# Transducer joint kernel: the second feature projection and two more groups of joint tiles computed by seven block products

## The chip, the cores and the metric

The kernel runs on one core of a Trainium2 chip. The metric is the time of one execution on the device in microseconds; the kernel before was run three times: 251.55, 252.01 and 252.47 us, median 252.01.

The core's engines, as the profile names them: PE (matmul; PEld is its weight load), DVE (VectorE), ACT (ScalarE), POOL (GpSimd) and SP, which here only issues DMAs. Matmul results stand in PSUM, which has eight banks of 512 fp32 columns; ACT and DVE read them out ("evict" them) to SBUF.

## What is computed

```python
h  = conv5(x, w1)                       # x: (2, 4000, 512), five taps, 512 -> 512
h  = gelu(h)[:, ::2, :]                 # (2, 2000, 512)
f  = gelu(conv5(h, w2))[:, ::2, :]      # (2, 1000, 512)
fe = f @ w_f                            # (2, 1000, 512)
ge = g @ w_g                            # (2, 8, 512)
j  = tanh(fe[:, :, None, :] + ge[:, None, :, :])   # (2, 1000, 8, 512)
out = j @ w_o                           # (2, 1000, 8, 512), bf16
```

All data are bf16. The joint part is the last two lines: 16,000 rows (16 pairs of batch and label position, 1000 rows each) through a 512 x 512 matrix.

## The kernel before

**Convolutions.** The first 216 rows of the first layer are done tap by tap; the rest of both convolutions runs in 24 *units* u0 to u23 (class Unit): six stretches of rows, four blocks of 128 output channels each. A unit has five steps, s1 to s5, of one or two products each; ACT applies GELU to their results. Units u16 to u19 make the features of the first batch (fT[0]) and u20 to u23 those of the second (fT[1]) from hT[1].

**Feature projection.** feT[b] = w_f applied to fT[b]. For the first batch the class Feature (L1001) does it by *seven block products*: both matrices are halved in both directions and seven products of half-size blocks take the place of eight, at the price of sums and differences of blocks. `wfsums` (L996) makes four sums of blocks of w_f (tile fs); `Feature.sums` (L1011) makes four of fT (tile ft); the methods p1 to p7 then do a product each for two blocks m of 128 output channels. Results that are needed twice are copied to sn, and added on DVE to later ones. For the second batch `fe` (L717) does it plainly: eight calls, four matmuls of 501 columns each, one eviction each, on ACT for odd m and on DVE for even m.

**Joint.** `tanh` on ACT makes j from feT and geT, up to 1000 columns at a time, into the rings jT and jX. The 16,000 rows are 125 tiles of 128. A tile is done in one of two ways:
- class Plain (L844): four matmuls of 512 columns into one bank, one eviction to ost, one store of 128 KB. `half` does half of the columns, two halves make a tile.
- class Seven (L873): four tiles at a time, a *group*. Four sums of blocks of j (`Seven.sums` L889, tile ss, on DVE or POOL), then seven products of four matmuls with 256 columns each, against blocks of w_o or their sums (tile tw, `wosums` L988). The bank A takes products 1, 6, 7 and 4 one after the other, the bank D products 5 and 3. Of the seven evictions three are copies to sn (s1, d5, u2; on ACT or DVE), three are additions on DVE to og (c11, c12, c22) and one is a copy to og (c21). A group is stored in two halves of 256 KB.

Before, 29 groups cover 116 tiles (L1135 to L1140) and nine tiles are plain: two at the start of the joint part, two after the 22nd group, two after the 28th, three at the end, the last of them in halves.

**What sets the order of the work.** The code issues operations in a logical order and derives every dependence from the cells that each one reads and writes. The order on each engine is not that of the code: it is read from a table, ORDER (L69), with one string for each engine. Each pair of letters is an operation's number; the table also says on which engine an operation runs that may run on two (evictions on ACT or DVE, sums on DVE or POOL). `schedule` (L198) reads it, `emit` (L210) adds the semaphores. The engines go through their lists strictly in that order. In the code's own order, `piece` (L1108) takes the next step of the list conv (what is left of the units, then the projection of the second batch) and puts it between the steps of the groups; `fill` (L1146) says how many go with each group.

**Ends.** The last three tiles (L1180 to L1195): one plain tile, the first half of the last, product 4 of the last group, the middle tile in halves, the second half of the last, whose eviction ACT does. SP issues all stores, in the table's order.

Of the kernel before, what the change touches and what calls it, by code (L numbers as in the profile page):

```python
# [63 lines left out]
class Op:  # L64
# [6 lines left out]
        "0X0Y0Z0a0b0c0d0e0f0h0j0l0t0u0v0w0x0y0z0_0-101112131415161g1718192C2c1A1i2J1j2K2m2E2e2n2f2F2x2v2M2N2j2p2k302q2y313334"  # L71
        "36373O3J3K3t3H3X3P3R3S3U3h3e3V3Z3a3i414A423k3v3l3_3w4K4C4D4L3f3-4Y444a454b4i4H4I4v4N4O4f4l5L4o4j5p4g4q5V4r4w4y4z4-4m"
        "505z5S5N5_5W5O6N5r5Y5Z5s5T6O6L6l606Y615w6Z6V5x6v6S6w786W6s6T6n6o7R7I6t7A7B7b6y7J7p7c7F6z7L7G7T7Y7U7r7Z7s7e7f7M807z81"
        "7_8T838m8A7w857x8B868D8E8n8d8e8V8W8r8a8t8G8u8g8H8h8-8o908p8y8z9D9F8b9G929N9K939Q9R9L9T9U9O9f9o9h9j9k9y9v9q9xA3A7A2A0"
        "A9ABAHAKAEAIAfANAgALASAiAjAlAmAPAvAwBGAoApB7B8AyBABBB0AzBgB1BQBTBDBHBRBhBEBmBJBUBKBnBdBpBqBjBsBkBXByCEBYC7BzCFBeB-C8"
        "CKCLCHCQCIC3CRC0CNC4CgCZCcCaCtCuCmCdChCzDACODBCnCwC_D3CxDLD0DPDQD1DSD4DHDVDIDbDDDTDcDEDYDlDiDmDWDZDjDvE6DwE3E4DpEZEC"
        "E7E0E1EDEaEQE9DqEJEKEUEAEMEVEREcEdENEfEiErEjEgEsF2EyEuFGFHFAEzElEvFJFBFDFKFdFEFSFMFTFZFaFVFjFWFkFpFsFmFnFvFqF-GNG2G0"
        "G3FtGEG6G7GFGjGKGHGLGOGkGIGWGQGXG-GdGeH0GsGmGnGpGZGqGaHCHLHDGvGtHIHFHGHJH2H6H7HUHMHjHkH3HVHXHOHbHcHmHsHYHtHpHnHzH_Hq"
        "IMIGIjIHINIPI0IkIJIKIQI4IdIpI1I5IWIZIXIqIeIzIaJCI_ImInJDJ4JfJIJJJFIsJGJSJ0JgJ5ItJ1JLJZJVJTJWJoJMJpJvJiKAJjJwKJKBJlJa"
        "JyKGJzJmKHKDKQKEKnKRKKKhK0K1KqKiKTKrKULALBKxKkKoKyKXKlLJLKKYLDLQLRLGK_K-LEL2LHLjLgL3LdLeLhLTLXLmLkLULwLYLnM9LxLpMILz"  # L80
        "L_M3M4MAMFMCMGMDMJMjMkMLMVMSMpMTMZNCMqMaMsNDMWMzMmMnNIM_NhNLNiMtN0NSN4NTNJNFNGN1NnN5NkNoNxNyNMNlO2NVNWO8NZNqNrOBOCN_"
        "N-O3OENaO9OHOIOFOkOlOOOPOROVOWOSOeP3P4OhObOfOcOnOuOvP9OiPAOxOyP6PCP7O-PJP0PFPKPMPNPDPTPUPQPRPXPaPdPePhPjPm"),
    "act": (
        "080k1L1F0m1N1s1o1y1R1Q1P1B1_1C1h1D2D2d1q1a1k2L1E1c2o2S2w2O2i2l2I2U2r2X352W2-323B383I2Y3Y3T3Q3p3u3D3n3j3W3o4B434S3N3d"
        "4M404Z3m3z3g464P4U5M4p4k544J4e4G5q52534_4h5-5X4n4x65514u5a5U6m6M71675y5R5K6-5v6X6a6R6U626x79707S7K7j7H7d5o6u7l6_5J7q"
        "7g6K7N6r827a7-7E848U6D8O5n5h7v6J7X8C8F6k898f7y8s6j8N978I8P918q778_8Z9E8c6d8i8x999M9S949V9J9P9g9p9i9z9r9nA49-AZA6ADAG"
        "AbAOAMAaAeAcAqAQB6AdAJB5BiBSCpCABLCsCCBVBtCBCrCDB_C9BfDOCqC1CbCvDND-CeB4CoCUDCD_DMDREYEXF8DdDnD5F4F5FgDzF7FfEEGCELFh"
        "EWF9GiFiGDF6EtHgEwFCHfFeIEFNHiIFFlGhHhG4G1JAK7GlJBGYIhIBGbK6IAGwK8K9HKHlJdHPIDICKdH-HrIOIlIiKbI2IrIbI-JeKgJKJhJ2KfJX"
        "L9JxKcL8JnM8KeKIKjM7LCMhLcKpLSMgLIL0LfLbLlNfLqLyNBN8MfMHNgMUNAMrNEMXN9M-NjNUNpNKNzMiNXO7O0OAOQO6OTOdP5OoPBOzPGPOPYPf"
        "PkPn"),  # L90
    "dve": (
        "000g0i1I1J1m1M1K1O1n1l1w1r1p1x1v1G1S1z1X1H1-1U1T2Q1V1W1Y1u1Z1b1f2R1d2G1e2H2g2P2h1t2T2z2t2V2_2b2Z2a2s3L3M3C392u3A3q3G"
        "3b3E3F3c493r3s3x4R473y4E4c4d4F4Q4T484V4s4t555d4W64574X565P5c66725t7P6P635u5Q5b5G5H5g5k6Q5E6A7Q69735F685I6p7i6G756q5i"
        "7C7D745l6B5f7O7k5j7V7W5m7t6c6H7h6C7o6E7u6F7m6g6I6e7n6h6b76876f888X8Q6i8S8Y8R8v8w988k8j9C8l969a9W9H9I959e9Y9B9Z9A9t9s"
        "9b9u9l9m9w9_A8A5A1AAACAFAXAVAWATAhAkAtBOAxAnArBMAsB9BCA_B2BIBFB3BoBrCVCWBlBuBZBvCGCMCJCSCTDeC5CPDfCiDhC-CyD9EFD2DUDJ"
        "DFDXDkDaDxDyE5E8E2FODrEBEbEOEeEhESF3EkE_EmFIF_FFFLFUFbGyFoFXFrFwFuGGG8GMGJGPGRGfH1JQHTHvGrGoHEGuHHH8H4HWHNHdJtHZHuHo"
        "ISIvITIIILI6IYIRIfIoJEJPJHJ6JsJUIuJNJkJqKCJ_JbKFKSK2KLKtKVKzKmKZKsLFLPLtL4LiLLMOLZLVLoM5MBMEL-MKMlMMMbMoMxNOMuNPNtNH"
        "N2N6NNNmNuNsNvNwOKODOGOJNbO4OXOgOsOwOjOmP8P1PLPEPVPSPbPi"),
    "pool": (
        "01020304050n0o0p0q20210r0s5e8M9X9d9cAYAuBNCXBPBwD8BxCYDgD6D7EHEGEnEIEoEpEqFxFQFyFPFzFRGSGTGVGUGxG_GzHQHRIxHSHwHxKOHy"  # L100
        "IUKvIwIVJOJrIyKMJuLMJRKNKPLsKuLNKwLvMvLOLuMwMPMRMyMQNRNQOLOMONOqOrOt"),
    "sp": (
        "0607090A0B0C0D0E0F0G0H0I0J0K0L0M0N0O0P0Q0R0S0T0U0V0W22232425262728292A2B58595A5B5C5D8J8K8LARAUA-BWBaBbBcC2C6CfCjCkCl"
        "DGDKDoDsDtDuEPETExE-F0F1FYFcG5G9GAGBGcGgH5H9HAHBHaHeI3I7I8I9IcIgJ3J7J8J9JYJcJ-K3K4K5KWKaL1L5L6L7LWLaLrM0M1M2M6MNMYMc"
        "MdMeN3N7NYNcNdNeO1O5OUOYOZOaOpO_P2PHPIPPPWPZPcPgPlPo"),
# [178 lines left out]
def bass_standalone__seq2seq_rnn_t_joint__speech_kernel(  # L284
# [22 lines left out]
    NK = D // P  # L307
# [3 lines left out]
    NT3 = (T2 + 2) // 3  # L311
# [5 lines left out]
    NT = 512  # L317
    NWARM = 8

    with ExitStack() as es:  # L320
# [396 lines left out]
        def fe(b, half, m):  # L717
            q = NT3 // 2
            v = ps.cols(bank(), 3 * q)
            mm(v, [(wf_sb[k, m * P:(m + 1) * P], fT[b][k, :, half * q:(half + 1) * q]) for k in range(NK)], True, True)  # L720
            v = v.map(lambda a: a.rearrange("p (r q) -> p q r", r=3))
            o = feT[b][m, 3 * half * q:3 * (half + 1) * q].map(lambda a: a.rearrange("p (q r) -> p q r", r=3))
            if m % 2:
                act(o, v, ACT.Copy)
            else:
                pl.op("dve", lambda e, o=o, v=v: e.tensor_copy(out=o.ap, in_=v.ap), (v,), (o,), vec_cost(o, (v,)))  # L726

# [268 lines left out]
        def wfsums():  # L996
            a11, a12, a21, a22 = (wf_sb[2 * k:2 * k + 2, m * H:(m + 1) * H] for m in range(2) for k in range(2))
            for i, x, y, op in ((0, a21, a22, add), (1, fs[0], a11, sub), (2, a11, a21, sub), (3, a12, fs[1], sub)):
                shared(fs[i], x, y, op, True)

        class Feature:  # L1001


            def __init__(self, b):
                self.b = b
                lo = (slice(0, FQ), slice(NT3 - FQ, NT3))
                self.B = {(k, n): fT[b][2 * k:2 * k + 2, :, lo[n]] for k in range(2) for n in range(2)}
                self.r = {1: (0, 0), 2: (1, 0), 3: (1, 1)}
                self.bk, self.kept = {}, {}

            def sums(self, late):  # L1011
                f = self.B
                for i, x, y in (((1, f[1, 1], ft[0]), (2, f[1, 1], f[0, 1]), (3, f[1, 0], ft[1])) if late else ((0, f[0, 1], f[0, 0]),)):
                    shared(ft[i], x, y, sub, False)

            def product(self, i, m, start):
# [7 lines left out]
                if lhs is None:  # L1024
                    s = {5: 0, 6: 1, 7: 2, 3: 3}[i]
                    lhs = lambda k: fs[s, k, c]
                if i in self.r:
                    kh, n = self.r[i]
                    lo = n * (NT3 - FQ)
                    rhs = lambda k: fT[self.b][2 * kh + k, :, lo:lo + FQ]  # L1030
                else:
                    t = {5: 0, 6: 1, 7: 2, 4: 3}[i]
                    rhs = lambda k: ft[t, k]
# [66 lines left out]
        wfsums()  # L1100
# [5 lines left out]
        conv += [lambda h=h, m=m: fe(1, h, m) for m in range(NK) for h in range(2)]  # L1106
# [40 lines left out]
        Plain(plains.pop(0)).go()
        Plain(plains.pop(0)).go()
# [31 lines left out]
        if len(plains) == 3:  # L1180
            Plain(plains[0]).go()
            end = Plain(plains[2])
            end.half(0, "dve", "sp")
            seven[-1].p4()
            Plain(plains[1]).halves()
        else:
            for j in plains[:2]:
                Plain(j).go()
            seven[-1].p4()
            for j in plains[2:-1]:  # L1190
                Plain(j).halves()
            end = Plain(plains[-1])
            end.half(0, "dve", "sp")
# [31 lines left out]
```

## Time and profile before

| | |
|---|---|
| runs, median (lowest to highest) | 252.01 us (251.55 to 252.47) |
| profiled execution, whole time | 251.88 us |
| its span, first to last instruction | 250.1 us |
| mean granted TensorE clock | 0.997 |
| matmuls with 256 columns | 828 |
| additions og <- acc, sn on DVE | 87 |
| sums ss on DVE, on POOL | 42, 74 |
| tanh on ACT from one pair and 128 channels | 64, in 84 pieces |
| last matmul ends, in the span | 246.44 us |
| median time from the issue of a 256 KB store to its landing | 2.2 us |

How to read it: the page gives the busy time of each engine as a share of the span, the chain of work that ended last, followed back from the last instruction, and the costliest groups of instructions. A group's line names the source line, the engine, the operation, the tiles (written <- read), the shape and the number; helpers record most operations, so that the matmuls all have line L411, DVE's additions L397, ACT's activations L403, copies of results L826 (ACT) and L827 or L831 (DVE), sums for groups L895 and the other shared sums L983. A record's duration includes latency that overlaps the next record; the time from one start to the next is what an engine that never waits spends on an operation.

### The profile page before, as it was taken

To read this page: it belongs to the slowest core of one execution; us is meant where nothing else is said; L and a number is where in the kernel's file an instruction comes from. 1 tells how busy PE (TensorE), PEld (TensorE's weight loads), DVE (VectorE), ACT (ScalarE), POOL (GpSimd) and SP (SyncE) were. 2 spreads that over 40 slices of the span, in tenths; PEclk is the share of its full clock that TensorE was granted. 3 is DMA by queue.
4 is the path that set the end of the run, shared out by engine and by line. 5 is a ranking of instruction groups with operands and counts; after the bars stand their busy time and mean duration, and the time that the engine had idled before them with its cause. 6 is when DMAs were issued, how large, how long until landed. Compare 5 with 4: busy or idle time off the path is not lost.

```text
span 250.1 us, 5178 instructions
## 1 busy us (share of the span) xinstructions
PE 244.3 (98%) x1912; PEld 184.1 (74%) x1916; DVE 216.3 (86%) x376; ACT 207.6 (83%) x351; POOL 90.1 (36%) x96
## 2 busy tenths in 40 slices
PE   8999999999999999999999999999999999999994
PEld 4556888887666666666558787877878888888873
DVE  1699989775999999799979867988999999979982
ACT  2199699848669398987899989999999999997853
POOL 1000000000000000001414494999857988695730
PEclk9999999999999999999999999999999999999998
DMA  7999999982900520000001123323333445564377
GB/s 218 323 205 181 184 164 185 165 144 84 321 19 3 182 70 3 1 1 3 0 0 66 63 87 127 126 87 128 126 116 116 141 161 187 168 197 164 100 251 240
DMA packets 57392, 31.92 MB, mean 128 GB/s; under 512 B 33837, under 2 KB 57149, under 8 KB 57367
## 3 DMA queue, kind: packets, MB, share of 16 engines
q1 hardware_dynamic: 57367, 31.59, 48.3%
q8 instruction: 15, 0.25, 0.4%
q14 instruction: 10, 0.08, 0.1%
HBM read 7.71 MB, written 16.38 MB: 96 GB/s over the span
## 4 chain that ended last, share of the span: by engine, by line
PE 98%; ACT 0%; issue 0%; DVE 0%
PE acc L411 97%; PE acc L489 1%; ACT xs L403 0%; ACT ost L403 0%; DVE zero L418 0%
## 5 line engine op out<-in xcount | busy, mean ns | idle before, releaser
L397 DVE TENSOR_TENSOR og<-acc,sn 128x512 bf16<-128x512 f32 x87 | 57.2, 684 | 6.5 <-PE acc L411 6.2
L411 PE MATMUL acc<-tw,ss 128*128 128x256 f16 x348 | 54.1, 273 | 0.0
L403 ACT ACTIVATE jT<-feT,geT 128x1000 bf16<-128x1000 f32 (+6 forms) x56 | 51.2, 950 | 0.4 <-DVE feT L726 0.3
L411 PEld LDWEIGHTS acc<-tw,ss 128*128 128x128 f16 x348 | 33.7, 98 | 6.7 <-ACT sn L826 0.3
L826 ACT ACTIVATE sn<-acc 128x512 f32<-128x512 f32 (+1 forms) x56 | 32.5, 617 | 4.8 <-PE acc L411 4.7
L411 PE MATMUL acc<-wo_sb,jT 128*128 128x256 bf16 (+1 forms) x192 | 33.8, 286 | 0.4 <-ACT jT L403 0.3
L411 PE MATMUL acc<-row,w_sb 128*128 128x334 bf16 (+1 forms) x192 | 32.1, 295 | 0.0
L411 PE MATMUL acc<-row,w_x 128*128 128x262 bf16 (+1 forms) x192 | 28.8, 290 | 0.0
L393 POOL MEMSET hT<- 128x8 bf16 (+2 forms) x6 | 0.7, 149 | 76.2 <-ACT hT L403 71.0
L403 ACT ACTIVATE sd<-acc 128x334 f32<-128x334 f32 (+1 forms) x48 | 19.9, 430 | 8.2 <-PE acc L411 7.8
L895 POOL TENSOR_TENSOR ss<-jT 128x512 f16<-128x512 bf16 x20 | 23.6, 1183 | 6.4 <-ACT jT L403 3.5
L403 ACT ACTIVATE jX<-feT,geT 128x1000 bf16<-128x1000 f32 (+4 forms) x28 | 25.1, 937 | 0.0
L411 PEld LDWEIGHTS acc<-row,w_sb 128*128 128x128 bf16 x192 | 18.5, 97 | 6.4
L411 PEld LDWEIGHTS acc<-row,w_x 128*128 128x128 bf16 x192 | 18.5, 98 | 6.1 <-ACT sd L403 0.4
L411 PEld LDWEIGHTS acc<-wo_sb,jT 128*128 128x128 bf16 x196 | 18.9, 98 | 5.2 <-ACT jT L403 0.4
L895 POOL TENSOR_TENSOR ss<-jT,ss 128x512 f16<-128x512 bf16 x15 | 17.3, 1158 | 11.7 <-DVE ss L895 11.5
L403 ACT ACTIVATE hT<-acc 128x262 bf16<-128x262 f32 (+2 forms) x36 | 15.2, 433 | 6.1 <-PE acc L411 6.1
L411 PE MATMUL acc<-wo_sb,ss 128*128 128x256 bf16 x116 | 20.3, 273 | 0.0
L827 DVE COPY sn<-acc 128x512 f32<-128x512 f32 x27 | 18.3, 684 | 1.4 <-PE acc L411 1.3
L500 DVE SCALAR_TENSOR_TENSOR acc<-acc,sd 128x334 f32<-128x334 f32 (+1 forms) x24 | 11.6, 485 | 6.6 <-ACT hT L403 3.2
L411 PE MATMUL acc<-hT,w_sb 128*128 128x334 bf16 x96 | 17.1, 305 | 0.0
L411 PE MATMUL acc<-row,w_t 128*128 128x334 bf16 x96 | 16.6, 305 | 0.0
(120 smaller groups left out, 503.8 us busy)
## 6 DMA issues: line engine op xcount, KB each, us to landing
out_dram<-og SPq DMA_DIRECT2D x44, 256.0 KB, 2.2
w_sb<-in_w_dram SPq DMA_DIRECT2D x9, 512.0 KB, 5.2
out_dram<-og SPq DMA_DIRECT2D x14, 128.0 KB, 2.2
out_dram<-ost SPq DMA_DIRECT2D x7, 128.0 KB, 2.2
xr<-in_x_dram SPq DMA_DIRECT2D x1, 512.0 KB, 3.6
w_sb<-in_w_dram SPq DMA_DIRECT2D x2, 256.0 KB, 4.8
wf_sb<-in_w_f_dram SPq DMA_DIRECT2D x1, 512.0 KB, 3.6
wg_sb<-in_w_g_dram SPq DMA_DIRECT2D x1, 512.0 KB, 4.6
```

The costliest lines, as they stand in the source:

```text
L393: pl.op("pool", lambda e: e.memset(v.ap, 0.0), (), (v,))
L397: pl.op(eng, lambda e: e.tensor_tensor(out=o.ap, in0=a.ap, in1=b.ap, op=op), (a, b), (o,), 0.02 + 2.14e-3 * o.ap.free_size() if eng == "po ...
L403: pl.op("act", lambda e: e.activation(o.ap, i.ap, func, scale=scale, bias=0.0 if bias is None else bias.ap), rd, (o,), o.ap.free_size() * ...
L411: ins = e.matmul(o.ap, lhsT=l.ap, rhs=r.ap, start=start and n == 0, stop=stop and n == len(pairs) - 1, skip_group_check=not check)
L489: ins = e.transpose(pv.ap[:, r, k, :], xr[rt].h[0:n, 2 * r + pp, k, :], ident.h[0:n, 0:n])
L500: pl.op(eng, lambda e: e.scalar_tensor_tensor(out=o.ap, in0=a.ap, scalar=f, in1=b.ap, op0=ALU.mult, op1=add), (a, b), (o,), vec_cost(o, (a ...
L826: pl.flex({"act": (lambda e: e.activation(o.ap, v.ap, ACT.Copy), 0.05 + n * 0.833e-3), "dve": (lambda e: e.tensor_copy(out=o.ap, in_=v.ap) ...
L827: "dve": (lambda e: e.tensor_copy(out=o.ap, in_=v.ap), 0.065 + n * 1.04e-3)}, (v,), (o,))
L895: fn = lambda e, o=S[i], x=x, y=y, op=op: e.tensor_tensor(out=o.ap, in0=x.ap, in1=y.ap, op=op)
```

## The change

Three things change; the convolutions and everything before the joint part are the same.

1. The projection of the second batch is done by the class Feature too. The function `fe` goes. ft and fs become lists of two; the second pair lies in hT[1], whose rows are read last by units u20 to u23. `wfsums` is called a second time for the second pair.
2. The groups begin at tile 0 and cover 124 tiles in 31 groups. One plain tile is left, the last one, in two halves. The steps "p" that put plain tiles between groups go.
3. The order table is another one. It has 1700 operations for 1651.

```diff
-        ft = at("ft", [4, 2, 3, FQ], BF16, ss[1].end - ss[1].bytes)
-        fs = at("fs", [4, 2, NT // 2], FP16, ss[3].end - ss[3].bytes)
-        assert ft.end <= ss[2].end
+        ft = [at("ft0", [4, 2, 3, FQ], BF16, ss[1].end - ss[1].bytes), at("ft1", [4, 2, 3, FQ], BF16, hT[1].end - hT[1].bytes)]
+        fs = [at("fs0", [4, 2, NT // 2], FP16, ss[3].end - ss[3].bytes), at("fs1", [4, 2, NT // 2], FP16, ft[1].end)]
+        assert ft[0].end <= ss[2].end and fs[1].end <= hT[1].end
...
-        conv += [lambda h=h, m=m: fe(1, h, m) for m in range(NK) for h in range(2)]
+        f1 = Feature(1)
+
+        for m in range(2):
+            conv += [lambda m=m: (f1.p1(m), m or (f1.sums(False), wfsums(fs[1]), f1.sums(True))),
+                     lambda m=m: (f1.p5(m), f1.p2(m)), lambda m=m: (f1.p6(m), f1.p3(m), f1.c12(m)),
+                     lambda m=m: (f1.p7(m), f1.p4(m))]
...
-        S1 = 15
-        gaps = (6, 12)
-        NEND = ntile - (2 + 4 * S1 + 4 * 14 + 2 * len(gaps))
-        jts = [2 + 4 * i for i in range(S1)]
-        j = 2 + 4 * S1
-        for n in range(14):
-            jts.append(j)
-            j += 4 + 2 * gaps.count(n)
-        assert jts[-1] + 4 < ntile
+        jts = [4 * i for i in range(ntile // 4)]
+        NEND = 1
         seven = [Seven(j) for j in jts]
-        plains = [j for j in range(ntile) if not any(q <= j < q + 4 for q in jts)]
-        fill = ["cc"]*9+["c"]*6+["p"]*15
-        Plain(plains.pop(0)).go()
-        Plain(plains.pop(0)).go()
+        plains = [ntile - 1]
+        fill = ["cc"]*9+["c"]*6+[""]*16
...
-        if len(plains) == 3:
-            Plain(plains[0]).go()
-            end = Plain(plains[2])
-            end.half(0, "dve", "sp")
-            seven[-1].p4()
-            Plain(plains[1]).halves()
...
+        end = Plain(plains[0])
+        end.half(0, "dve", "sp")
+        seven[-1].p4()
         end.half(1, "act", "sp")
```

Operations of the joint part by engine, counted in the two tables:

| | before | after |
|---|---|---|
| PE, products of 256-column blocks (two matmuls each) | 406 | 434 |
| PE, 504-column products (two matmuls each) | 14 | 28 |
| PE, 501-column products (four matmuls each) | 8 | 0 |
| PE, plain tiles: 512 columns / 256 columns (four matmuls each) | 7 / 4 | 0 / 2 |
| DVE, 512-wide additions / copies | 87 / 49 | 93 / 42 |
| DVE, feature additions / copies (501 and 504 wide) | 6 / 6 | 12 / 4 |
| DVE, sums for groups / for features / of weights | 42 / 4 / 5 | 57 / 8 / 8 |
| ACT, 512-wide copies / feature copies | 74 / 10 | 82 / 12 |
| POOL, sums for groups / of weights | 74 / 3 | 67 / 4 |
| SP, stores | 97 | 94 |

More of the change, by code (lines that the diff above doesn't have):

```diff
@@ L70 @@
     "pe": (
[L71 to L82, printed above, removed]
@@ L83 @@
-    "act": (
[L84 to L90, printed above, removed]
@@ L91 @@
-    "dve": (
[L92 to L98, printed above, removed]
+        "0X0Y0Z0a0b0c0d0e0f0h0j0l0t0u0v0w0x0y0z0_0-101112131415161718191g1A2C2c1i1j2m2v2J2n2K2E2F2x2e2f2y2M2p2N362q333O2j3730"
@@ new lines @@
+        "34312k3H4A3X3J3K3t3R3P3S3h3i413Z423a3e3f4C4D4K3v3U4N3w3V3k4L3_3l4Y444a4b453-4H4o4O4i4l4m5L4j4I5p4q4r4y5V4f4z4v4-5W4g"
+        "6L4w5S5N5O505z5r5s5_5T6l6N5Y5w5Z5x6O786v6V606W6S617I6Y6T7J6w6Z6s6n6o7T7A6t7p7B7R6y7U7L7F7M6z7G7e7f837b7Y7c7Z7z7r7_8D"
+        "7w8E85867s8T8V80818A7x8m8d8W8B8e8n8o8a8r8t8G8b8H8g8-8h908p8u8y9D9F8z929K9G9N939O9f9Q9R9L9T9U9h9o9v9xA09y9qA3A7ANA9A2"
+        "9jAiAEAj9kABB1AZAwAxAHAaB2AKALAIApAcAdAfBDAqBVBABEBWAsB4AgB5BKBkAtBYBBB7BLBZBNBOB8BeBfBhBqBrBbBcBRC8BSCBBzC9C1C2BiCE"
@@ new lines @@
+        "CTCUCFBtBuCCCHCoCICpB_CaCWCbCXCKCLD5DJClCmDKD6DFCxCuCyCvD2CrD3DVCsDWCeCfDBDMDNDCDnDPDcDQDdDfDuDoDvDjDgDxE4DyDkEODSEB"
+        "DTE5EEEFE1ETEZE2EUEaD_D-ECEPEfE_EKE-EcEWELEtEuEXEdF2FCF4FFEwExFGFQFOFxFDFrFsFZFIFyFWFXFJFjG7FaFuFLFvFfFMG8FgGEFlGFGA"
+        "GBGKG1GTGLGNF_F-GUGOGYGeGtGQGRGWH3GfGzGuG_GhGnGwGxGiH5HBHYHEH0HCH1GoHFHxHMHPHNHVHaHSHTHIHQHJI1HgI2HhHyHjHWHpIYHqHkH_"
+        "IBICH-ISI4I5IxIbITIZIIIVIcIJIWIEIiIyIjJ1JOJPIFIrIsJ2JBJCJUJVI_JeI-JIIlJfJJJRImJEJSJ4JnJFJtJuJ5JoJXK0KMK7K8JhJYJwKNJi"
@@ new lines @@
+        "JxJzJ_K1KSKTKtKuKPKEKFKcKVKQKWKdKAKzLKK_KlLLKBKfKgL7LELaL8LFL0KmKwKxLQL1LbLRLNLpLALBLOLTLqLsLtMILjMJLUM3LkM4LvLyLzLd"
+        "MYLeLwMZM6M7MlMRMrMmMOMLMPMAMMMBMSMuM-N0MsMfMgMoMpNGNHMbMcNMN6MvN7NNNJNKNWN2N3OENPNlNmOFNXNZNrNdNaNeNQN-O0NsNoNuNpNv"
+        "OUOKOLOHOhOVOiO2OnO3OoOIO6OxO7OyObOcOkOqOlP8ONOrP9OOOXP2PBPCOYPEP3O_POO-PPPHPFPZPRQ0PSPcQ1PdPaPIPVPfPiPWPgPjPpPqQCQD"
+        "PsPwPxPtQ3Q4Q6Q7Q9QJQAQFQGQKQMQNQQQTQUQX"),
+    "act": (
+        "080k0m1o1N1L1q1R1Q2S1P1s1B1y1h1_2d1C1k2D1a1D2o2L1c2w1F1E2U2r2O2W2X35382Y2l3Y2i3I323B3u3T2I433D3N4B3j3g3n3d3o3W3Q4M2-"
+        "3z3m3p464Z404S5M4P4k4p4U4J544n5q4e4_535X524h4G4u654x6M515-6-6m5U5R5a5v796X5y6762716x5o7K706a5K6U6R7S7q5h6u6r7N5J6_5n"
+        "7j777E7H847d6K7a6D7l7-8F6J8U7v827g7X8O7y6k8C6d8f8N8s6j8P978I8c919E8x8Z8_8q898i99949S9M9J9V9i9p9z9rA49PAO9-ATA6AkAUAD"
+        "AGAVAWAMAYA-BFAXC6AJC4B0CjChBaB9BlBPBsC7BXC5CVDIC3DHCYCiCkDtDGDLESDsFAD7DXA_9nCgERCzDeF8COFoDwF9DhGsF6E6DrFpEVEQF7EG"
+        "FnEgEvF3FqEyFBFEFPFtFYGIGJG9FbFmGCHtGrG2IQHuGXGgH4IMJrGjIvIPIRHOHUHvI3HzIOHlHwIDKKIwJNIkIzINJQJsJDJWKqJgInKLJGJvJMKr"
+        "K9LIKOKUKpKvKIK-LMKCKhL9LoLnLcLSKsMGLJM5KJLfNELxM8MnMHMaMkMtNhN1MdMjNjNCNOOGNnNYN4O1NtNiNDOMNFO4NkOpODOCPAOZOfOgPGP0"
+        "PTPbQ2PhPrQEPuQ8QHQVQY"),
@@ new lines @@
+    "dve": (
+        "000g0i1I1m1J1M1O1n1l1K2Q1u1p1r1w1H1v2R1z1U1S1T1x1V1W1-1Y1X1G1Z1b1t2P2G1d2g2T2z1e2_2H1f2h2V2Z2b2a392s3L2t3C2u3A3M3q3b"
+        "3F3E4E3c3G3x484F3y3r3s474c4Q494T4R4d4s4V554W4X4t5d5c56575b5P6c5t5u5Q5G646A5k5E5f6P73766Q5l5H6672636b685F5g696g5I7Q6C"
+        "5i6p5j757C6q6G7V7P7D747W5m6B7i7O6H6E7k7h7o7n6F6I7t7u7m6e87886h8X8Y6f8Q8R8k8S6i8l968j988v8w9C9Y9H9c9e9I9W959X9g9A9Z9b"
+        "9s9t9d9wA19u9_A8AAA59BAFAC9l9mAyAbAPAQASB3AzAeAnAlArAhB6AuBCBMBoBmBgBJCPBTBnCABdBjCGCDC_CqCcBvCMCNCJB-CnE9CSDYD4CtD1"
+        "E7CwEpE8EqDODRDDDpDqErEsDlDzDUEiEhE3EbE0EDEnEmFSEMEYF5F0FHEeEoFTG3FVFKFkFzFwFRFhFNGGGMG0GVGZGPGSGvG-GyH6HZHDH2GpHGHb"
+        "HRHKHiHXHrIeJ7IfI8I0IUI6IKIaIXIdJ3ItIGJ0JKK4JaJ9JbK6JTJ6JpJZJjJ-K2JyKGKRL4KZKaKbL-L6KeKXKnKyLGL2LPLrLCMKLlLuL_LVMWLZ"
+        "MVMxM1MQMCMNMTMhNIMqN8NLMwNSNxNTOQNyNVNRNfNqNwNbOjOWOJO8OzOdOmOPPDP4OsPQOwPKPlPLPmPePJPkPXPyQ5PoQBQLQOQR"),
@@ L99 @@
     "pool": (
-        "01020304050n0o0p0q20210r0s5e8M9X9d9cAYAuBNCXBPBwD8BxCYDgD6D7EHEGEnEIEoEpEqFxFQFyFPFzFRGSGTGVGUGxG_GzHQHRIxHSHwHxKOHy"
-        "IUKvIwIVJOJrIyKMJuLMJRKNKPLsKuLNKwLvMvLOLuMwMPMRMyMQNRNQOLOMONOqOrOt"),
+        "01020304050n210o200p0q0r0s5e8M9aARBIBGAmBHAoBpCQC-D0CRDaDZEADbFUEjElG5GaEkH7GbH8G4H9G6GcHcHeGdHAHdI7HfI9IAJ8IhK3IgJA"
+        "JdJcKYK5L3M0LWL5LXLYM2MUMyMXNUM_MzN_NzOROSOTOtOuPnOvPNPM"),
     "sp": (
-        "0607090A0B0C0D0E0F0G0H0I0J0K0L0M0N0O0P0Q0R0S0T0U0V0W22232425262728292A2B58595A5B5C5D8J8K8LARAUA-BWBaBbBcC2C6CfCjCkCl"
@@ L104 @@
-        "DGDKDoDsDtDuEPETExE-F0F1FYFcG5G9GAGBGcGgH5H9HAHBHaHeI3I7I8I9IcIgJ3J7J8J9JYJcJ-K3K4K5KWKaL1L5L6L7LWLaLrM0M1M2M6MNMYMc"
-        "MdMeN3N7NYNcNdNeO1O5OUOYOZOaOpO_P2PHPIPPPWPZPcPgPlPo"),
+        "0607090A0B0C0D0E0F0G0H0I0J0K0L0M0N0O0P0Q0R0S0T0U0V0W22232425262728292A2B58595A5B5C5D8J8K8LAvBQBUBwBxByC0CZCdD8D9DADE"
+        "DiDmEHEIEJENEzF1FcFdFeFiGDGHGkGlGmGqHHHLHmHnHoHsIHILIoIpIqIuJHJLJkJlJmJqKDKHKiKjKkKoLDLHLgLhLiLmM9MDMEMFMeMiN5N9NANB"
+        "NcNgO5O9OAOBOaOeP1P5P6P7PUPYPvPzP_P-QIQPQSQWQZ"),
@@ L715, in ge @@
             act(geT[:], ps.cols(c0, NK * BU), ACT.Copy)
[L717 to L726, printed above, removed]
         def slot(j):
@@ L994, in wosums, with wfsums @@
             shared(tw[3], b21, tw[1], sub, True)
-        def wfsums():
+        def wfsums(fs):
             a11, a12, a21, a22 = (wf_sb[2 * k:2 * k + 2, m * H:(m + 1) * H] for m in range(2) for k in range(2))
@@ L1004, in __init__ @@
             def __init__(self, b):
-                self.b = b
+                self.b, self.ft, self.fs = b, ft[b], fs[b]
                 lo = (slice(0, FQ), slice(NT3 - FQ, NT3))
@@ L1011, in sums @@
             def sums(self, late):
-                f = self.B
+                f, ft = self.B, self.ft
                 for i, x, y in (((1, f[1, 1], ft[0]), (2, f[1, 1], f[0, 1]), (3, f[1, 0], ft[1])) if late else ((0, f[0, 1], f[0, 0]),)):
@@ L1025, in product @@
                     s = {5: 0, 6: 1, 7: 2, 3: 3}[i]
-                    lhs = lambda k: fs[s, k, c]
+                    lhs = lambda k: self.fs[s, k, c]
                 if i in self.r:
@@ L1032, in product @@
                     t = {5: 0, 6: 1, 7: 2, 4: 3}[i]
-                    rhs = lambda k: ft[t, k]
+                    rhs = lambda k: self.ft[t, k]
                 mm(ps.cols(bk * NT, 3 * FQ), [(lhs(k), rhs(k)) for k in range(2)], start, True, False)
@@ L1099, in bass_standalone__seq2seq_rnn_t_joint__speech_kernel @@
         pl.hold.append(mark)
-        wfsums()
+        wfsums(fs[0])
         wosums()
@@ L1179, in bass_standalone__seq2seq_rnn_t_joint__speech_kernel @@
         assert not conv and not pend and len(plains) == NEND, (len(conv), len(pend), plains)
-        if len(plains) == 3:
-            Plain(plains[0]).go()
-            end = Plain(plains[2])
-            end.half(0, "dve", "sp")
-            seven[-1].p4()
-            Plain(plains[1]).halves()
[L1186 to L1193, printed above, removed]
+        end = Plain(plains[0])
+        end.half(0, "dve", "sp")
+        seven[-1].p4()
         end.half(1, "act", "sp")
```

## The prediction

> **What bounds the kernel now.** I read the page's busy shares, then the chain that ended last in order of time, then busy time by stage, then the timeline of each engine.
>
> Busy shares and the chain's shares (page):
> ```profile
> PE 244.3 (98%) x1912; PEld 184.1 (74%) x1916; DVE 216.3 (86%) x376; ACT 207.6 (83%) x351; POOL 90.1 (36%) x96
> PE 98%; ACT 0%; issue 0%; DVE 0%
> ```
> The chain in order of time (start, duration, what):
> ```profile
> 128.56 0.26 issue
> ...
> 246.44 0.02 issue
> 246.46 0.38 ACT ost L403
> ```
> PE sets the end: from 7.64 to 246.44 the chain is PE alone but for gaps of 0.26, 0.05, 0.05 and 0.05 us. 3.7 us of store follow the last matmul.
>
> Busy time by stage of the joint part (stretch: length, PE, PEld, DVE, ACT, POOL, clock, DMA):
> ```profile
> 129.00:165.00 36.00, 36.00 (x294) 28.38 (x293) 29.96 (x56) 35.09 (x57) 24.83 (x22) 1.00 0.25 82
> 165.00:215.00 50.00, 50.00 (x429) 41.34 (x428) 47.22 (x84) 49.68 (x78) 40.17 (x37) 1.00 0.44 143
> 215.00:246.50 31.50, 31.26 (x266) 25.66 (x266) 27.97 (x50) 24.78 (x43) 19.40 (x17) 1.00 0.57 185
> ```
> PE is full at clock 1.00, but DVE and ACT stand close behind. A busy record overlaps the next one, so I sum by steps (start to start) from the timeline:
> ```profile
> 122.07 1.01 PE L411 MATMUL acc<-ft,fs 128*128 128x504 bf16 x4
> 173.88 0.60 PE L411 MATMUL acc<-wo_sb,ss 128*128 128x256 bf16 x4
> 240.82 0.81 PE L411 MATMUL acc<-wo_sb,jT 128*128 128x512 bf16 x3
> 130.27 1.28 DVE L827 COPY sn<-acc 128x512 f32<-128x512 f32 x2
> 131.47 0.75 DVE L895 TENSOR_TENSOR ss<-jT 128x512 f16<-128x512 bf16 x2
> 118.64 1.55 ACT L826 ACTIVATE sn<-acc 128x504 f32<-128x504 f32 x3
> ```
> One record lasts 0.375, 0.273, 0.379, 0.68, 0.417 and 0.59 us, so the steps are 0.212 us for a 504-column matmul, 0.109 for 256 columns, 0.2155 for 512, 0.60 for a 512-wide DVE eviction, 0.335 for a DVE sum, 0.48 for ACT. A POOL sum steps at 1.115. The 256-column step is the same over the whole joint part, so fewer columns mean less time.
>
> **The change, part by part.** The order table's letter pairs are operation numbers (64 x first + second); numbering the operations as the code issues them tells which engine each one is on and what stands around it.
>
> *PE.* Two more groups of four tiles: 56 matmuls of 256 columns, +6.10. Gone: seven whole plain tiles, 28 of 512 columns, -6.03, and one tile done in halves, 8 of 256, -0.87. Second projection: 32 of 501 columns go, -6.78, and 28 of 504 come, +5.94. **PE: -1.64 us**, all on the chain as long as PE gets its operands in time.
>
> *DVE.* From the two tables: 15 more sums for the groups (57 for 42, +5.0), 6 more 512-wide additions (+3.6), 6 more feature additions (at 0.643, +3.9), 4 feature sums (0.595, +2.4), 3 weight sums (+1.0), 2 more feature copies (+1.2), against 7 copies fewer (-4.2), four 501-wide ones (-2.3) and a half (-0.3): **+10.2 us**. ACT: +8 copies (+3.8), +6 feature copies (+2.9), -4 (-1.9), -0.3: +4.6. POOL: -7 sums, +1 weight sum: -6.7. None is on the chain before; PE covers them. Over the whole joint part, steps summed, PE takes 128.8 before and 127.2 after, ACT 116.1 and 120.7, DVE 110.9 and 121.0.
>
> That cover nearly goes. Take a DVE operation that reads a product, and set what DVE still has to do from there against what PE still has to do. Some 46 us into the joint part, at an eviction of the sixth group, before: DVE 73.3, PE 82.9, room 9.6. After, at the seventh group's first addition (also 46.7 us in): 104 plain 512-wide ones (62.2), 36 sums (12.1), 6 feature additions (3.9), the rest 2.7: 80.8, against 82.2 on PE. Room 1.4, and it stays between 1.0 and 1.4 until 113 us in. For ACT the room is 2 to 3.5 us (8 to 10 before).
>
> Small costs eat this room. Over all operations that follow another at once, the 512-wide step is 0.604, not 0.598: +0.6. Of 42 DVE sums 32 met no POOL sum and last 417 ns; ten met one and last 503 on average (longest 764): 20 ns each over all, +0.7. So DVE needs 82.1: room 0.1. Then every wait of DVE in this stretch is paid in full. One can be named: the feature sums of the second batch are queued on DVE behind the last GELU of the second convolution, which comes some 0.3 us late; behind them stand the group sums. How much of DVE's present idling stays can't be read off:
> ```profile
> DVE og L397 <- PE acc L411: 6.2, 12, 1.3
> DVE ss L895 <- ACT jT L403: 1.8, 2, 1.1
> ...
> PEld acc L411 <- ACT jT L403: 0.4, 1, 0.4
> ```
> (who waits for whom: total, times, longest; joint part). All of DVE's waits there sum to some 12 us, out of the 18 by which its work was short of PE's. Bounds for what is left of them after: 0 and 12. I take 0.6, near the half microsecond that PE itself waits now, since both are then engines without room. **DVE: +0.1 + 0.6 = +0.7.**
>
> *The sums' buffers* of the second batch lie in hT[1]; what overlaps is read last by the products of u23's s0, 45.4 us in, before DVE comes to it: nothing, or up to 0.3 if PE is late there.
>
> *The start.* The 0.26 us gap is the first plain tile waiting for the fifth tanh. After, no plain tile stands there. By the steps, the first group's first sums are ready 15.3 us after the first feature product starts, and PE comes to them at 15.9, having units 20 and 21 in front: **-0.26**, at worst +0.5.
>
> *The tail.* Before, the last store is issued 0.6 us after the last matmul, behind one store; SP's issues:
> ```profile
> 245.83 0.62 SPq L943 DMA_DIRECT2D out_dram<-og  x1
> 246.55 1.49 SPq L841 DMA_DIRECT2D out_dram<-ost  x2
> ```
> After, a group's product stands second to last, only 0.44 us of PE time before the end. Its ACT copy ends about 0.2 after the last matmul, its 256 KB store takes SP some 0.62, and the last half tile's store waits behind it until about 0.95: **+0.35** (0 to 0.6). Fewer issues in all (94 for 97) change nothing.
>
> **Sum:** -1.64 + 0.7 - 0.26 + 0.35 = -0.85. The profiled run took 251.88 (span 250.1 and 1.8 around it), which gives 251.0; the median of the runs, 252.01, lies 0.13 higher. **Forecast 251.2 us.**
>
> A rule speaks against this. The Trainium skill, page SBUF — State Buffer, section "SBUF: two separate sides", says that a DVE operation with two SBUF inputs and a GpSimd operation that reads SBUF hold their shared ports exclusively, and that the later one stands still until the other is done. By it, a DVE sum that meets a POOL sum would wait up to the 1.16 us that one lasts; the trace shows 0.35 us at most and 86 ns on average, for ten meetings. What it would do here is priced from those rows as the second rival.
>
> **Rivals.** *Full gain:* DVE's room holds, no wait is left: -1.64 - 0.26 + 0.2 = -1.7, 250.3. For it: PE waited only half a microsecond in all before. Against: DVE's room of 0.1.
>
> *DVE takes over (slower).* Place: the 80 us from the seventh group on. DVE then has 36 sums, and POOL is busy most of that time (40.17 of 50 now). If 22 of them meet a POOL sum at 0.17 us each (the mean excess of the five longest in the trace), that is 3.7, less the 0.7 counted: +3.0, so 254.2. It decides against the change from 1.6 us on top of the forecast. For it: 22 more DVE operations with two SBUF inputs than the trace shows, and no room. Against: POOL has six sums fewer, and three quarters of the sums met none.
>
> *Handed back:* the lost waits come to about what PE saves: 251.9. For it: the same rows, milder.
>
> That the work isn't saved can be left out: the numbers of operations in the tables agree with the matmuls counted above.
>
> **How the numbers follow.** Forecast 0.35, full gain 0.17, handed back 0.22, DVE takes over 0.26. About 0.3%, 0.76 us, is what a measurement of this kernel can tell from no change: under 251.25 is faster, over 252.77 slower. Full gain and some three quarters of the forecast's cases are faster (0.43), the rest of them and the handed back ones the same (0.31), the last slower (0.26). The range runs from full gain with no tail cost, -1.9, and 0.1 below it, 250.0, to DVE taking over with three quarters of its price, 253.5; half of that rival lies beyond.
>
> **What would show it.** Right: the chain is PE up to the last matmul, DVE's busy share is 91 to 92%, DVE shows nearly no idle time between 165 and 240 us, PE's gaps sum to a microsecond, and the last store is issued 0.9 us after the last matmul. Wrong towards slower: the chain changes to DVE for many microseconds, DVE sums above 0.5 us, PE waiting on sn, og or ss. Wrong towards faster: DVE idles a few microseconds and PE has no gaps.

## The result, and the profile after

| | before | after |
|---|---|---|
| median of six runs (lowest to highest) | 251.62 us (251.55 to 252.47) | 250.58 us (250.48 to 251.08) |
| profiled execution: whole time, span | 251.88, 250.1 | 250.51, 248.7 |
| last matmul ends | 246.44 | 245.14 |

The ratio of the means is 0.9955 (95% interval 0.9942 to 0.9968). The medians differ by 1.04 us, the means by 1.15: **about 1.1 us faster**, by 0.45%. The forecast's sum was 0.85 us faster, its time 251.2 us. Three more runs of the kernel before brought its median from 252.01 down to 251.62.

Busy shares and the chain's shares, from the page of the changed kernel (its line numbers are one higher in the upper part of the code):
```profile
PE 243.2 (98%) x1932; PEld 183.9 (74%) x1932; DVE 223.8 (90%) x400; ACT 210.4 (85%) x360; POOL 83.1 (33%) x90
...
PE 71%; DVE 16%; DMA 5%; ACT 3%; issue 3%; ACTq 0%; DVEq 0%
```
PE is 98% busy as before, though the chain now gives it only 71%. The chain in order of time says why:
```profile
110.80 0.77 DVE hT L398
111.56 0.43 DVE acc L501
111.99 0.05 issue
112.04 132.68 PE acc L412 x1104
```
From 112.0 to 244.7 us the chain is PE without a break. Just before, PE lost 0.22 us to a wait for DVE's acc (one step of 0.365 us in place of 0.142), and a chain that is followed back leaves PE at such a wait, however short it was; it comes back to PE only for 95.5 to 99.7 and 23.1 to 62.6 us. Its share of PE fell, though PE is as busy as before.

Busy time by stage (stretch: length, PE, PEld, DVE, ACT, POOL, clock, DMA), to be read against the three lines of before:
```profile
129.00:165.00 36.00, 36.00 (x299) 28.89 (x298) 33.11 (x65) 35.18 (x58) 19.10 (x17) 1.00 0.25 81
165.00:215.00 50.00, 50.00 (x434) 41.50 (x433) 49.81 (x91) 50.00 (x81) 39.84 (x36) 1.00 0.44 143
215.00:245.00 30.00, 30.00 (x274) 26.17 (x272) 29.57 (x57) 28.04 (x49) 19.27 (x17) 1.00 0.58 189
```
Three engines are full at once between 165 and 215 us; DVE had 47.22 of 50 there before. Who still waits for whom between 118 and 249 us (total, times, longest), DVE's largest wait and PE's:
```profile
DVE og L398 <- PE acc L412: 1.5, 3, 1.1
...
PEld acc L412 <- ACT sn L816: 0.9, 4, 0.3
PEld acc L412 <- DVE og L398: 0.6, 3, 0.3
```
DVE's waits for its additions fell from 6.2 us in 12 to 1.5 in 3. Of the prediction's signs, DVE's idle time between 165 and 240 us (0.5 us, before 4.7) and the last store's issue (0.97 us after the last matmul) came as said; DVE's busy share is 90%, where 91 to 92% was expected, and the chain is PE alone only from 112 us on.

**Where the time went, in PE's own steps.** I took the time from the first matmul with 334 columns (48.2 us in both) to the start of the last one, and summed what each matmul's step exceeds its usual step by (PE's waits):

| us | before | after | e4 (below) |
|---|---|---|---|
| first 334-column matmul to last matmul | 197.93 | 196.66 | 196.35 |
| of it PE's waits up to 118 us | 0.06 | 0.51 | 0.06 |
| PE's waits from 118 us on | 0.38 | 0.42 | 0.46 |
| last matmul's start to the end | 3.94 | 3.82 | 3.84 |

Less waits, before is 197.5 and e4, which has the same order up to the joint part, 195.8: PE's work fell by 1.66 us, and 1.64 was forecast. A better order alone could not have given this: in the kernel before PE's waits in that stretch sum to 0.44 us, and the stretch became 1.27 us shorter. (After itself comes to 195.7: in the old order before the joint part one step of a 16-column matmul, at 100.7 us, lasts 0.12 us instead of 0.025, which the new order doesn't have. The column of before leaves out four matmuls whose records are missing, 32 of 36 with 512 columns being there: they look like gaps of exactly one 512-column step, 0.216 us. Three of the four gaps that the prediction read off the chain, those of 0.05 us, are such holes, and a fourth record is missing behind the 0.26: from start to start PE lost 0.42 us there, 0.22 of it the record and 0.2 the wait.)

### The profile page after: what moved, and what is told of

Its sections match the earlier page's. It is cut to its first block, busy times and chain, and to the rows that moved or that the text cites. A ratio compares the mean times of both kernels' runs of the same rounds, so it can differ in the third digit from the quotient of the medians.

```text
span 248.7 us, 5273 instructions
## 1 busy us (share of the span) xinstructions
PE 243.2 (98%) x1932; PEld 183.9 (74%) x1932; DVE 223.8 (90%) x400; ACT 210.4 (85%) x360; POOL 83.1 (33%) x90
## 4 chain that ended last, share of the span: by engine, by line
PE 71%; DVE 16%; DMA 5%; ACT 3%; issue 3%; ACTq 0%; DVEq 0%
PE acc L412 71%; DVE row L398 5%; DMA w_sb<-in_w_dram 4%; DVE ssum L501 3%; DVE ssum L398 2%; DVE w_t L398 1%; DMA xr<-in_x_dram 1%; DVE xp L398 1%; ACT row L404 1%; ACT hT L404 1%; DVE acc L501 1%; DVE hT L398 1%; DVE w_sb L398 1%; DVE sd L398 1%; DVE w_x L398 1%
## 5 line engine op out<-in xcount | busy, mean ns | idle before, releaser
L398 DVE TENSOR_TENSOR og<-acc,sn 128x512 bf16<-128x512 f32 x93 | 59.4, 681 | 2.1 <-PE acc L412 1.5
L412 PE MATMUL acc<-tw,ss 128*128 128x256 f16 x372 | 58.1, 273 | 0.0
L816 ACT ACTIVATE sn<-acc 128x512 f32<-128x512 f32 (+1 forms) x68 | 41.2, 676 | 2.1 <-PE acc L412 2.0
L412 PEld LDWEIGHTS acc<-tw,ss 128*128 128x128 f16 x372 | 35.6, 98 | 6.9 <-ACT sn L816 0.3
L885 POOL TENSOR_TENSOR ss<-jT 128x512 f16<-128x512 bf16 x22 | 25.1, 1158 | 21.5 <-ACT jT L404 17.5
L412 PE MATMUL acc<-wo_sb,jT 128*128 128x256 bf16 x176 | 30.0, 273 | 0.0
L412 PE MATMUL acc<-wo_sb,ss 128*128 128x256 bf16 x124 | 22.0, 273 | 0.0
L412 PEld LDWEIGHTS acc<-wo_sb,jT 128*128 128x128 bf16 x176 | 17.0, 98 | 3.3
L817 DVE COPY sn<-acc 128x512 f32<-128x512 f32 (+1 forms) x27 | 18.3, 681 | 0.5 <-PE acc L412 0.5
L816 ACT ACTIVATE og<-acc 128x512 bf16<-128x512 f32 x25 | 16.2, 667 | 1.7 <-PE acc L412 1.7
```

The costliest lines, as they stand in the source:

```text
L398: pl.op(eng, lambda e: e.tensor_tensor(out=o.ap, in0=a.ap, in1=b.ap, op=op), (a, b), (o,), 0.02 + 2.14e-3 * o.ap.free_size() if eng == "po ...
L412: ins = e.matmul(o.ap, lhsT=l.ap, rhs=r.ap, start=start and n == 0, stop=stop and n == len(pairs) - 1, skip_group_check=not check)
L816: pl.flex({"act": (lambda e: e.activation(o.ap, v.ap, ACT.Copy), 0.05 + n * 0.833e-3), "dve": (lambda e: e.tensor_copy(out=o.ap, in_=v.ap) ...
L817: "dve": (lambda e: e.tensor_copy(out=o.ap, in_=v.ap), 0.065 + n * 1.04e-3)}, (v,), (o,))
L885: fn = lambda e, o=S[i], x=x, y=y, op=op: e.tensor_tensor(out=o.ap, in0=x.ap, in1=y.ap, op=op)
```

## The experiments

Each ratio is to the kernel before on the same chip; after itself has 0.9955. Where a kernel differs in the order table, I say which operations stand elsewhere.

### e1 and e5: the second projection plain again

```diff
-        f1 = Feature(1)
-        for m in range(2):
-            conv += [lambda m=m: (f1.p1(m), m or (f1.sums(False), wfsums(fs[1]), f1.sums(True))),
...
+        def fe(half, m, bk):
+            v = ps.cols(bk * NT, 3 * q)
+            mm(v, [(wf_sb[k, m * P:(m + 1) * P], fT[1][k, :, half * q:(half + 1) * q]) for k in range(NK)], True, True)
...
+        for m in range(2):
+            conv += [lambda m=m: fea(m), lambda m=m: feb(m), lambda m=m: fec(m), lambda m=m: fed(m)]
```
In the table the eight calls stand in the places of eight of the fourteen feature products, their evictions in the places of those products' evictions. e5 differs from e1 in these places alone, which moves one eviction from DVE to ACT.

> Undoes the first part of the change alone: the second batch's projection is plain again (eight calls of four 501-column matmuls in the places of the feature products, in the same banks), the 31 groups stay. PE gets 0.84 us more (32 x 0.212 against 28 x 0.212), DVE 4.8 us less, ACT 1.4 us less. Theory 'columns' (PE's work alone sets the end, the fuller DVE costs a few tenths): 0.84 us slower than the changed kernel, ratio to the kernel before 0.998 to 0.9995. Rival 'no room' (DVE is a bound of its own in the joint part): the relief of DVE pays PE's columns back, ratio 0.995 to 0.997.

> The second batch's projection plain again, as in e1, with other places in the order: the last call of each half stands in the place of product 6 and is evicted by ACT, so that no tanh waits for an eviction late in DVE's list (in e1 ACT stood 2.2 us at one tanh and PE 1.7 us behind it). Theory 'columns': 0.84 us of PE more and few waits, 0.8 to 1.5 us slower than the changed kernel, ratio to the kernel before 0.9985 to 1.002. Rival 'no room': 0.995 to 0.997. Third theory 'any other order than the found one costs microseconds, whatever the engines' work': ratio above 1.005.

Measured: e1 1.0106 (1.0088 to 1.0124), e5 1.0074 (1.0051 to 1.0097): 3.7 and 3.2 us slower than after, e1 outside both of its theories. In e5 PE's waits from 118 us on are 2.71 (after 0.42), so of 3.2 us some 0.8 is columns and 2.3 is waits, with 4.8 us less work on DVE. Stages of e5:
```profile
165.00:215.00 50.00, 48.91 (x411) 38.95 (x410) 43.11 (x80) 46.59 (x74) 35.48 (x32) 1.00 0.39 128
```
DVE and ACT stand idle, 6.9 and 3.4 us, and still PE waits for them. The time fits the third theory: a table made for other operations costs more than the operations. The 0.8 is counted from the columns. What the relief of DVE is worth by itself the run doesn't show, since the waits of the unsuited order cover it; so it neither confirms nor refutes "no room".

### e2 and e6: four groups done plainly

```diff
+        class Four(Seven):
+            def tile(self, t, bk, eng):
+                mm(ps.cols(bk * NT, NT), [(jcols(k, (self.jt + t) * P, P), wo_sb[k, :]) for k in range(NK)], True, True)
+                evict(eng, self.o[t], ps.cols(bk * NT, NT))
...
-        seven = [Seven(j) for j in jts]
+        seven = [(Four if i in (15, 18, 21, 24) else Seven)(j) for i, j in enumerate(jts)]
```


> Undoes part of the second part of the change: four of the 31 groups (the 16th, 19th, 22nd and 25th) do their four tiles plainly (four matmuls of 512 columns a tile, one eviction a tile, the same buffers, banks and stores). PE gets 4 x 0.40 = 1.6 us more; DVE loses four additions, copies and sums, some 7 us. Theory 'columns': 1.3 to 1.6 us slower than the changed kernel, ratio to the kernel before 1.000 to 1.002. Rival 'no room': at most 0.5 us slower than the changed kernel, ratio 0.995 to 0.9975.

> Four groups done plainly, as in e2, with other places: the tiles' products stand at products 2, 6, 3 and 4 of the group and each eviction in the place of that of the same bank (in e2 PE stood 2.1 us at one late eviction). Theory 'columns': 1.6 us of PE more, ratio to the kernel before 1.000 to 1.004. Rival 'no room': 0.995 to 0.9975. Third theory 'order': above 1.010, PE waiting again by several microseconds although DVE has 7 us less to do.

Measured: e2 1.0302 (1.0273 to 1.033), e6 1.0107 (1.0084 to 1.0131). Between the two only the places of the four groups' products and evictions (and with them the engine of some evictions) differ, and the times differ by some 5 us. Both lie outside "columns" and "no room". In e6, 3.7 us more lie between the first 334-column matmul and the last matmul than after: 1.6 of columns, 1.9 of waits in the joint part, 0.2 of waits before it. The same reading as e5.

### e3 and e7: sixteen sums from POOL to DVE, in the changed kernel and in the kernel before

Only the table is edited: sixteen evenly chosen sums for groups leave POOL's list and stand in DVE's list before the operation that ran next when POOL began them.

> Sixteen of the 50 sums that POOL does for the groups between 165 and 236 us are moved to DVE: 16 x 0.34 = 5.4 us more DVE work there, the rest of the order as it was. The prediction's account (room 0.1, every microsecond of DVE paid in full): 5 us slower than the changed kernel, ratio to the kernel before 1.013 to 1.018. Theory 'room is what the trace shows as DVE's idle time', about 2 us in that stretch: 2.5 to 4 us slower, ratio 1.004 to 1.012. Theory 'columns' in its strong form (DVE is covered): no change, ratio 0.995 to 0.997.

> The kernel before with sixteen of the 49 sums that POOL does between 165 and 236 us moved to DVE, in the way of e3, which made the changed kernel 10.3 us slower. DVE gets 5.4 us more. Theory 'room' (DVE had 5 to 8 us of room there before, hardly any after): the kernel before loses 0 to 2.5 us, ratio to itself 1.000 to 1.010. Rival 'order' (moving operations in a list costs by itself, whatever the room): about as much as in e3, 8 us or more, ratio above 1.030.

Measured: e3 1.0369 (1.0351 to 1.0388), e7 1.0218 (1.0192 to 1.0245): 10.3 and 5.5 us. Neither theory's number came out, because the load was larger than I had put it. A stretch of e3's timeline, DVE and then POOL:
```profile
211.08 1.38 DVE L886 TENSOR_TENSOR ss<-jT 128x512 f16<-128x512 bf16 x1
212.38 1.37 DVE L886 TENSOR_TENSOR ss<-jT,ss 128x512 f16<-128x512 bf16 x1
213.67 1.37 DVE L886 TENSOR_TENSOR ss<-jT 128x512 f16<-128x512 bf16 x1
214.96 0.41 DVE L886 TENSOR_TENSOR ss<-jT,ss 128x512 f16<-128x512 bf16 x1
```
```profile
210.88 3.88 POOL L886 TENSOR_TENSOR ss<-jT 128x512 f16<-128x512 bf16 x3 [2.97 <-ACT jT L405]
```
While POOL does three sums, three DVE sums last 1.37 us each, and 0.41 when POOL has stopped. In e3 20 of DVE's 73 sums met a POOL sum and lasted 745 ns on average, in e7 14 of 58, 803 ns; alone they last 416 to 420. So DVE got 5.4 us of sums and 6.3 (e3) or 4.6 (e7) of standing still more than its base kernel: 11.7 and 10.0. The last matmul came 10.6 and 5.3 us later, counted from the first 334-column one. The kernel before swallowed 4.7 us, the changed one 1.1. The prediction has a room of 9.6 us before at one place, the expectations 5 to 8 for this stretch, and 0.1 to 1.4 after: the direction agrees, the 4.7 is a little under the lowest of the figures for before, and e10 below gives far less.

### e4 and e8: the order before the joint part, and the last store

e4 puts the operations up to the joint part back into the order of the kernel before; the joint part keeps the new order. e8 is e4 with one more edit: the last store moves from SP's list to the end of ACT's.
```diff
-        end.half(1, "act", "sp")
+        end.half(1, "act", "act")
```


> The changed kernel with one thing undone: the operations before the joint part stand in the order of the kernel before, the joint part's order is the new one. Theory 'the new order before the joint part costs PE waits' (0.22 us at 95.2 and 0.25 at 111.7 in the trace after; none in the trace before): 0.3 to 0.5 us faster than the changed kernel, ratio to the kernel before 0.993 to 0.9945. Rival 'they are handed on': the joint part then waits by as much at its start, ratio 0.995 to 0.996.

> The kernel of e4 (old order before the joint part, new order in it) with one edit: the last store, of the last half tile, is issued by ACT right behind its eviction and no longer by SP behind a 256 KB store. In the trace after the eviction ends at 245.61 and SP issues the store at 246.11. Theory 'the tail is set by the last issue': 0.3 to 0.5 us faster than e4, ratio to the kernel before 0.992 to 0.9928. Rival 'the 256 KB store before it lands last anyway': no change, ratio 0.9935 to 0.9945.

Measured: e4 0.9941 (0.9927 to 0.9956), e8 0.9937 (0.9916 to 0.9959). The two waits of the trace after, at 95 and 112 us, are gone in e4 (0.06 for 0.51, table above). Who PE waited for between 85 and 118 us, in after and then in e4:
```profile
PEld acc L412 <- DVE acc L501: 0.6, 2, 0.4
...
PEld acc L412 <- ACT sd L404: 0.4, 1, 0.4
```
```profile
PEld acc L412 <- DVE acc L501: 0.2, 1, 0.2
```
All eight traces with the new order in front show both waits, at 0.2 us each, and none of the six with the old order does. The stretch up to the last matmul is 0.31 us shorter in e4 (196.35; e8, with the same PE list, has 196.33). The medians, 250.21 and 250.24 against 250.58, point the same way, but the intervals overlap with that of after: shown in the trace, not in the times.

e8 issues the last store 0.4 us earlier and ends no sooner. Its tail:
```profile
245.66 0.44 SPq L933 DMA_DIRECT2D out_dram<-og  x1
245.67 0.40 ACTq L831 DMA_DIRECT2D out_dram<-ost  x1
```
The 256 KB store from og, issued at 245.66, has its last packet at 247.75; that of the half tile landed at 246.99. In e4 the half tile's came last, at 247.65, right after the 256 KB one at 247.44. By the trace the rival was right: with the half tile's store out of the way, the group's store lands last, and no sooner. The time can't tell, since e8's interval holds both forecasts.

### e9 and e10: plain load on DVE

```diff
+        for i in range(6):
+            v = sd[i % 3][0:2]
+            pl.op("dve", lambda e, v=v: e.memset(v.ap, 0.0), (), (v,))
```


> The changed kernel with six memsets of 672 fp32 elements on DVE, on tiles that nothing uses any more, spread evenly from 168 to 232 us in DVE's list: about 3 us of plain load (0.5 us each by the 0.27 us of the 256-element memset in the trace), without moving any operation. The prediction's account (room 0.1 to 1.4 us, then paid in full): 1.5 to 3 us slower than the changed kernel, ratio to the kernel before 1.001 to 1.008. Theory 'covered': no change, 0.995 to 0.997. Theory 'each delay is paid at its place' (PE is late behind every one, room or not): 3 us or more, above 1.007.

> The same six memsets in the kernel before. The prediction's account (5 to 8 us of room there): 0 to 0.5 us slower, ratio to itself 0.998 to 1.003. Theory 'each delay is paid at its place': about what e9 loses, 2 to 3 us, ratio 1.008 to 1.013.

Measured: e9 1.0084 (1.0065 to 1.0103), e10 1.0084 (1.0068 to 1.0099). A memset steps at 0.535 us: 3.2 us of load in both. From the first 334-column matmul to the last one e9 needs 3.55 us more than after, e10 2.06 more than before. The changed kernel pays the whole load and a little more, which is past the upper end of the prediction's account (3 us, 1.008) and within the theory that each delay is paid at its place. The kernel before pays two thirds, where the account said 0 to 0.5: its room of 5 to 8 us took in 1.1 of 3.2, and its ratio lies at the lower end of the other theory's range. So most of the load was paid even where there was room; what the room can have saved is at most the difference between the two kernels, 1.5 us.

### e11 and e12: less work for PE alone

```diff
-                mm(ps.cols(bk * NT + t * H, H), [(lhs(t, k), rhs(k)) for k in range(2)], start and t == 0, True, False)
+                mm(ps.cols(bk * NT + t * H, H), [(lhs(t, k), rhs(k)) for k in range(1 if i == 7 and 14 <= self.n < 30 else 2)], start and t == 0, True, False)
```


> The changed kernel with PE's work alone made smaller: product 7 of sixteen groups (the 15th to the 30th) takes only the first 128 of its 256 inner elements, two matmuls of 256 columns fewer a group, 32 x 0.109 = 3.5 us; everything else, order, evictions and sums, stays. Theory 'PE's columns set the end': 2.5 to 3.5 us faster than the changed kernel, ratio to the kernel before 0.981 to 0.986. Rival 'DVE is as late as PE' (the prediction's room of 0.1 to 1.4 us): only 0.1 to 1.5 us of it comes out, ratio 0.9895 to 0.9955.

> The same in the kernel before: product 7 of sixteen groups (the 14th to the 29th) with half of its inner elements, 3.5 us less for PE. The prediction's account (5 to 8 us of room on DVE, 8 on ACT): nearly all of it comes out, 2.8 to 3.5 us, ratio to itself 0.986 to 0.989. Rival 'the lists are tied together everywhere': half or less, ratio above 0.993.

Measured: e11 0.9988 (0.9977 to 0.9998), e12 0.9973 (0.9957 to 0.9989). With 3.5 us less to do, PE ends 0.7 us *later* in the changed kernel and 0.9 us earlier in the kernel before. PE's waits from 118 us on rose to some 4.4 and 2.9 us (every matmul that the code issues is on record in both). Its largest ones from 165 us on, in e11:
```profile
PEld acc L412 <- ACT sn L816: 3.5, 14, 0.5
PEld acc L412 <- DVE og L398: 2.4, 7, 1.0
...
PEld acc L412 <- ACT og L816: 0.8, 3, 0.3
```
In the changed kernel none of PE's columns comes out: PE waits for ACT most, which the prediction had given 2 us or more of room, and then for DVE. e11 lies outside both of its theories; "DVE is as late as PE" fits its direction, but e12 shows that this is not the only reading. In the kernel before, with its room, a quarter came out, where nearly all was expected and the rival "the lists are tied together everywhere" said half or less. An order made for other durations thus loses most of the gain in both kernels. Why e11 is slower than after and not merely as fast stays open.

## Why the prediction was right, step by step

- **PE, -1.64:** measured 1.66 with waits taken out (before against e4). Steps from start to start and a count of matmuls are enough for this.
- **DVE, +0.7 (0.1 for the room, 0.6 for waits):** the direction held, the size was too large. Without the wait at the start, PE's waits in the joint part went from 0.18 to 0.42 us: +0.24. The step that was mis-sized is the 0.6 of waits, which no row gave. The statement behind it, that every DVE delay would be paid in full, came true in e9 (3.55 for 3.2); its reason, the missing room, is not shown by it, since the kernel before paid two thirds of the same load.
- **Room as a buffer:** here the prediction's reasoning failed, without harm to the number. It took "what DVE has still to do against what PE has still to do" for what a kernel can swallow. That sum is only a bound: e10 and e12 found far less in the kernel before. The reading that fits is that each list is followed strictly, so that an operation late by half a microsecond makes PE wait at its place, whatever idle time follows. It fits e5 and e6 too, which lost 2 us with engines idle; no run tests it apart from the rest.
- **The start, -0.26:** right. The wait for the fifth tanh is gone, and PE came to the first group's sums without waiting. The wait that went was 0.2 us in start-to-start steps.
- **Before the joint part, nothing:** wrong by +0.35. My text called everything before the joint part the same; the code is, but the table was found anew for all of it, and 168 of the first 218 operations in PE's list stand in another place. Two waits, for ACT's sd and for DVE's acc, cost 0.45, and e4 takes them away; with the 0.1 of the long 16-column step that the new order saves, the first feature product comes 0.35 us later than in e4, counted from the first 334-column matmul. I should have compared the tables up to the joint part as I did inside it.
- **The tail, +0.35:** the last store was issued 0.97 us after the last matmul's end, as forecast (0.95), but the tail got 0.12 shorter. Wrong step: that the end follows the last issue. Landing matters: before, the last packet landed 2.1 us after the last issue, after 1.6. Why is open: counted from the last issue, 382 packets of 1 KB were still to start before and 341 after; counted from the end of the last matmul, 526 and 637.
- **The feature sums late by 0.3:** DVE waited 0.5 us once for a product of the features; no wait of DVE for the second convolution's GELU shows. Small, and not separated further.

Sum of what was found: -1.66 + 0.35 - 0.2 + 0.24 - 0.12 = -1.39; the spans of the profiled executions differ by 1.40, their whole times by 1.37, the medians by 1.04. So PE's term was right, and around it errors of opposite sign stood: 0.35 left out in front, against 0.46 too much for DVE's waits and 0.47 too much for the tail. Against the traces the forecast gain is half a microsecond too small; that it lies only 0.2 us from the medians is luck in part. As a time, 251.2 is 0.6 us above the 250.58 measured, mostly because it started from 252.01, where six runs give 251.62.

The rival "full gain", -1.7, is not far off: the medians lie nearer to the forecast, the profiled executions nearer to this rival. It took DVE's room to hold and no wait to be left; of the 0.7 us that the forecast charged for DVE, 0.24 came, so the mechanism lies between the two, nearer to the rival. "Handed back" did not come.

The rival "DVE takes over" did not come in this kernel: 8 of 57 DVE sums met a POOL sum, at 445 ns, fewer than before (10 of 42, at 503). In seven of the eight DVE's sum began first and lasted its usual 0.41 to 0.42 us, and POOL's lasted 1.20 to 1.28 instead of 1.16. The rival's mechanism is real, as e3 shows, and at a higher price than the 0.17 us a meeting that it was given: 0.33 in e3. The Trainium skill, page SBUF — State Buffer, section "Who interferes with whom", has the rule: whichever of the two operations comes second stands still until the other is done. The trace of e3 agrees, with 1.37 us for a sum that takes 0.42 alone.

## What to carry to other kernels

Where every engine follows a fixed list, a sum of work by engine tells what a new order can reach, and a change of work without an order made for it tells little: here 3.5 us less for the busiest engine gave 0.9 us or none, and relieving another engine went with some 2 us more of waits. Compare the whole lists, also where the code is the same. And read the waits in the steps of the engine that binds, not in the chain's shares: PE's share of the chain went from 98% to 71% over waits of 0.2 us each.

## What the runs showed of the hardware that was not expected

- Two-input sums on DVE beside POOL's sums go in lockstep: 1.37 us for 0.42 (e3), and POOL's own sums stretch too, from 1.16 to between 1.28 and 1.33 us. In all fourteen traces every DVE sum for a group that lasted over 0.435 us ended 0.28 to 0.29 us after the POOL sum that it met.
- PE's start varies from trace to trace: the granted clock became full 6.3 us after the first instruction in the trace before and 4.7 us in that after (3.9 to 7.1 us over all fourteen traces), and the first convolution matmul came at 7.64 and 7.05 us. By 48 us the difference between before and after is gone (first 334-column matmul at 48.22 and 48.20): after has waits of its weight loads that before doesn't have, 0.46 us for DVE's row at 21 us and 0.37 us for ACT's w_x at 23 us.
- A missing matmul record looks like an idle PE for exactly one step (three gaps of 0.216 us in before, where 512 columns step at 0.2155). Such gaps are to be held against the number of matmuls that the code issues.
